# A fused retention and feed-forward kernel: another buffer and another queue for three blocks of output sums

## The chip, the cores and the metric

The kernel runs on one core of a Trainium2 chip. The metric is device time in microseconds (us) of one execution; smaller is better. The kernel before takes 835.1 us, the median of three runs (834.79 to 836.32).

## The reference

Two layers follow each other, all in float32. The first is a retention layer: for 8 batches, 8 heads, 576 positions and head size 64, the scores `q k^T / 8` are multiplied with a lower triangular matrix of powers of a decay that depends on the head, and with `v`. The second takes its output as `x`, 4608 tokens by 512:

```
a = x @ w1                     # 512 -> 1024
b = x @ w2                     # 512 -> 1024
out = ((a * b) @ w3) @ w_out   # 1024 -> 1024 -> 512
```

## The kernel before

**What is computed in which form.** The product `w3 @ w_out` (a tile called `w3o`, 1024 by 512) is made once, early. After that a block of tokens needs two large products: an "up" (`x` with `w1` and `w2`, then the elementwise product into a tile `ab`) and a "down" (`ab` with `w3o`). Both are done by a seven-product scheme (Strassen's form), so each needs sums of its operands, made by VectorE (DVE), beside the matmuls of TensorE (PE).

**Tokens.** The 4608 tokens are 12 blocks of 384, numbered m from 0. A block is cut into three pieces t of 128 tokens. One call `down(x, y)` works on two pieces, for instance x = (2, 2) and y = (3, 2): piece 2 of block 2 and piece 2 of block 3.

**What `down` does.** It makes seven products (L645) in the order 1, 7, 2, 6, 5, 4, 3, each of four matmuls, in PSUM. Product 1 is copied out by ScalarE (ACT, L679), product 2 continues in the bank of product 1, and ACT copies that too (L696). The others are added by DVE (L695, then `plus`, L649) into a tile `ot` of 128 partitions by 1024 elements. There is one buffer of `ot`. Product 3 continues in the bank of product 5, and so waits for the addition of product 5. After the additions `put` notes which rows of `ot` are whole and `store` (L723) sends them to the output. `store` takes ACT's queue unless it is told another. So the next `down` may write into `ot` only where its stores have landed, and everything that ACT has to do after a store stands behind that store's wait.

**Who fills the gaps.** `plus` also takes work out of lists that other parts filled: `spread` (sums on the weights and their sending, below), `pieces` (sums of tokens for the next stage, L966), and `aside` (among others the three sums that the next `down` needs: S3, S2, S1, lines 614, 618 and 620). One call of `plus` takes one entry of `spread` or else of `pieces`, and one of `aside`.

**The change of stage.** The first four blocks use weights that lie in SBUF (`wA`, `wS`). The later eight use a two-level form whose weight forms lie in HBM (`kept`) and come through a ring of three slots (`ra`, 896 KB each, L954). Between them, `weight_forms` makes the last sums on `wA` and `wS` (L885) and sends all forms to `kept` (L895, L898, L901), half by GpSimd (POOL), half by SyncE's queue (SP). Slots two and three of the ring lie in the space of a weight tile that has been sent, so their first loads wait for these sends to land. The first load is issued by SP (`open_first`), the second by SP (`open_second`), the third by ACT (`next_forms(nc.scalar)` near the end of the listing), and all later ones by POOL. The stage's matmuls are L1053: one `up2` for each slot.

**Order of the work around the change.** Three calls of `down` stand there, one after another in time, from about 319 to 363 us: first (1, 0) with (1, 1); second (2, 2) with (3, 2); third (3, 0) with (3, 1). After the first comes the last part of a retention chunk (`pv`, copies L306 on ACT), loads for the next chunks, and the scaling of `v` of the next chunk by its decays on ACT (L202, eight instructions). After the third come `front` (transposes L218, copies L221), `state` (L255, L259) and `score` (L233), and then the first `up2`. The order on every engine is the order in which the program is written down; the compiler adds waits on semaphores. Each DMA of SP or ACT is given one of eight semaphores in turn, each DMA of POOL one of eight others, and a DMA waits for the landing of the one that had its semaphore before.

Of the kernel before, what the change touches and what calls it, by code (L numbers as in the profile page):

```python
# [8 lines left out]
F32 = mybir.dt.float32  # L9
# [10 lines left out]
def kernel(  # L20
# [13 lines left out]
    nc = tc.nc  # L34
    moe_w1, moe_w2, moe_w3, moe_w_out = (
        w.bitcast(I32).rearrange("r (c t) -> r c t", t=2) for w in (moe_w1, moe_w2, moe_w3, moe_w_out))
    B, H, S, D = q.shape
    DM = H * D
    DF = moe_w3.shape[0]
    CV = 512  # L40
    P = 128
# [12 lines left out]
    TB = S // NB  # L54
    NT = 2 * TB // P
    KD = DM // P
    KF = DF // P
# [6 lines left out]
    ffn = ctx.enter_context(tc.tile_pool(name="ffn", bufs=2))  # L64
# [6 lines left out]
    pools = {}  # L71
# [123 lines left out]
    def scale(g, nm, scalar=False, engine=nc.gpsimd):  # L195
        c = g % NC
        sz = sizes[c]
        t, gam = live[nm, g], {"q": gq, "v": gk}[nm]
        t = t[:sz].rearrange("p (b h) d -> p b h d", b=2)
        if scalar:  # L200
            for h in range(H) if scalar is True else scalar:
                nc.scalar.mul(t[:, :, h, :], t[:, :, h, :], gam[:sz, c, h:h + 1])  # L202
            return
        engine.tensor_tensor(
            out=t, in0=t, in1=gam[:sz, c].unsqueeze(1).unsqueeze(3).to_broadcast([sz, 2, H, D]), op=ALU.mult)
# [366 lines left out]
    aside, owed, spread, beside, loads = [], [], [], [], []  # L572
    g = 0
# [31 lines left out]
    def pair_of(x, y):  # L605

        if (x, y) not in pairs:
            X, Y = tokens(*x), tokens(*y)
            a = {"A11": X[:, :NP], "A12": X[:, NP:], "A21": Y[:, :NP], "A22": Y[:, NP:],
                 "S3": Y[:, :NP], "S4": X[:, NP:]}  # L610

            def sums(nm):
                if nm == "S3":
                    nc.vector.tensor_tensor(out=a["S3"], in0=a["A11"], in1=a["A21"], op=ALU.subtract)
                elif nm == "S2":
                    forms = pools["forms"].tile([P, 2, NP, P], F32, tag="forms", name="forms")
                    a["S1"], a["S2"] = forms[:, 0], forms[:, 1]
                    nc.vector.tensor_tensor(out=a["S2"], in0=a["A22"], in1=a["S3"], op=ALU.subtract)
                else:
                    nc.vector.tensor_tensor(out=a["S1"], in0=a["S2"], in1=a["A11"], op=ALU.add)  # L620
                done.append(nm)

            done = []
            pairs[x, y] = a, done, [lambda nm=nm: sums(nm) for nm in ("S3", "S2", "S1")]
        return pairs[x, y]

    def ahead(x, y, n=3):
        todo_sums = pair_of(x, y)[2]
        for _ in range(min(n, len(todo_sums))):
            aside.append(todo_sums.pop(0))  # L630

    def down(x, y, then=None, last=False):
        a, done, left = pair_of(x, y)
        second = "first" in live
        early = second or last or g >= 2 * NC - 1
        ahead(x, y)
        while len(done) < (1 if second else 3):
            aside.pop(0)()
        ps = {}
        ot = pools["ot"].tile([P, 2, 2, DM // 2], F32, tag="ot", name="ot")  # L640

        def product(nm, A, B, on=None):
            ps[nm] = ps[on] if on else acc.tile([P, DM // 2], F32, tag="acc", name="po")
            for f in range(NP):
                nc.tensor.matmul(ps[nm], a[A][:, f, :], live["W"][B][:, f, :], start=(f == 0 and not on),  # L645
                                 stop=(f == NP - 1), skip_group_check=True)

        def plus(nm, to, sb):
            nc.vector.tensor_add(ot[:, to[0], to[1]], ps[nm], ot[:, sb[0], sb[1]])  # L649
            if spread:  # L650
                spread.pop(0)()
            elif pieces:
                pieces.pop(0)()
            if early and aside and nm != 3:
                aside.pop(0)()

        def put(m, t, row, half=slice(0, 2)):

            i, n = every[m]
            r0 = t * P  # L660
            while r0 < (t + 1) * P:
                b = r0 // TB
                e = min((b + 1) * TB, (t + 1) * P)
                r = (2 * i + b) * S + n * TB + r0 - b * TB
                stores.append((out[r:r + e - r0, half.start * DM // 2:half.stop * DM // 2],
                               ot[r0 - t * P:e - t * P, row, half].rearrange("p h d -> p (h d)")))
                r0 = e
            if not keep_stores and not second:
                store()

        C11, C12, C21, C22 = (0, 0), (0, 1), (1, 0), (1, 1)
        product(1, "A11", "B11")
        first = ot[:, 0, 0]
        if second and not steps[0]:
            first = live["spare"]
        elif second:
            first = live["first"].pop(0)
            live["first"].append(first)
        nc.scalar.copy(first, ps[1])  # L679
        if second:  # L680
            store()
            finish()
            if steps[0] and sent[0] < steps[0] + 3:
                next_forms()
        product(7, "S3", "T3")
        if second:
            multiply()
        while len(done) < 3:
            aside.pop(0)()
        if then:  # L690
            ahead(*then)
        product(2, "A12", "B21", on=1)
        nc.vector.tensor_tensor(out=a["S4"], in0=a["A12"], in1=a["S2"], op=ALU.subtract)
        product(6, "S2", "T2")
        nc.vector.tensor_add(ot[:, 0, 1], ps[6], first)  # L695
        nc.scalar.copy(ot[:, 0, 0], ps[2])  # L696
        if early:
            put(*x, 0, slice(0, 1))
            store()
        plus(7, C21, C12)  # L700
        product(5, "S1", "T1")
        plus(5, C22, C21)
        product(4, "A22", "-T4")
        plus(4, C21, C21)
        put(*y, 1)
        if second:
            store()
        product(3, "S4", "B22", on=5)
        while aside and not early:
            aside.pop(0)()  # L710
        plus(3, C12, C12)
        put(*x, 0, slice(1 if early else 0, 2))
        if last:
            store()
        while aside:
            aside.pop(0)()
# [3 lines left out]
    def store(engine=nc.scalar):  # L720
        while stores:

            engine.dma_start(*stores.pop(0))  # L723
# [125 lines left out]
    ahead((2, 0), (2, 1), 1)  # L849
    up(0, 2, NQ - 1)  # L850
    down((2, 0), (2, 1), ((0, 0), (0, 1)))
    carry(2, 2)
    weights_part.close()
# [6 lines left out]
    keep_stores.clear()  # L860
    store()
    todo = [(down, (0, 0), (0, 1)), (down, (0, 2), (1, 2))]


# [50 lines left out]
    ring, sent, steps, free = [], [0], [0], []  # L915
# [34 lines left out]
    def next_forms(engine=nc.gpsimd):  # L950
        n = sent[0]
        if n < 14 * len(groups):
            nm = NAMES.index(OPERANDS[order[n % 7]][0])
            engine.dma_start(ring[n % 3], kept[n % 14 // 7][nm])  # L954
            sent[0] += 1
# [57 lines left out]
    def finish():  # L1013
        while behind:
            behind.pop(0)()

    def multiply(most=2 * len(order)):
        while results and most:
            gr, h, f, b, z, s = results.pop(0)
            m = groups[gr][s]  # L1020
            if ("ab", *every[m]) not in live:
                live["ab", *every[m]] = ffn.tile([P, 2 * KF, TB], F32, tag="ab", name="ab")
            ab = live["ab", *every[m]].rearrange("p (q i) t -> p q i t", i=4)[:, 2 * h:2 * h + 2, 2 * f + b, :]
            v = z.rearrange("p (m s) w t -> p m s w t", s=2)[:, :, s]
            nc.vector.tensor_mul(ab, v[:, :, 0, :], v[:, :, 1, :])  # L1025
            if s == 0:
                free.append(z)
            most -= 1
# [99 lines left out]
    def work(n):  # L1128
        while n > 0 and todo:
            fn, *args = todo.pop(0)  # L1130

            nxt = next((x for x in todo if x[0] in real), None)
            if nxt and nxt[0] is down:
                if fn is down:
                    args.append(nxt[1:])
                else:
                    ahead(*nxt[1:], 1 if fn is up2 else 3)
            if g == G and not todo:
                fn(*args, last=True)
            else:  # L1140
                fn(*args)
            n -= 1
            while todo and todo[0][0] not in real:
                todo.pop(0)[0]()

    g = NC
# [49 lines left out]
    g = 2 * NC - 1  # L1196
# [3 lines left out]
    pv(g)()  # L1200
    load(g + 2, "v", nc.scalar)
    load(g + 2, "k")
    scale(g + 1, "v", True)
    open_first()
    token_forms(0)

    g = 2 * NC
    work(1)
    aside.append(lambda: scale(g, "q", True))
    work(1)  # L1210
# [55 lines left out]
    g = G  # L1266
# [44 lines left out]
```

## Time and profile before

| what | value |
|---|---|
| median of three runs | 835.1 us (834.79 to 836.32) |
| the profiled execution | 834.5 us |
| its span, from the first to the last instruction | 832.8 us |
| granted TensorE clock, mean | 1.0 |
| PE busy | 814.8 us, 98% of the span |
| DVE / ACT / POOL busy | 546.3 / 291.6 / 216.3 us |
| stores by ACT's queue, by POOL's queue | 59, 4 in all |
| a store's time from issue to landing, median | 2.3 us |

A view of the timeline has one row for instructions of one kind that follow each other: start in us from the span's start, length in us, engine, line, operation, tiles (out<-in), shape, count; in brackets, how long the engine was idle before and what ended that. ACTq and SPq are the sequencers of these engines, on which DMAs are issued. A line "DMA ... us to landing" counts from issue to landing. Since the issue is on an engine's own queue, a row of several issues includes the waits between them. PE's records overlap a little: a product starts before the modelled end of the one ahead.

### The profile page before, as it was taken

How to read it: one execution, taken by the hardware profiler on the slowest of the kernel's cores; microseconds unless marked ns; L12 is line 12 of the kernel's file. 1: busy time of each engine (PE TensorE's matmuls, PEld its weight loads, DVE VectorE, ACT ScalarE, POOL GpSimd, SP SyncE). 2: the span in 40 equal slices, each digit the busy share in tenths (PEclk: the TensorE clock that was granted, in tenths of full speed). 3: DMA queues.
4: the chain of work that ended last, by engine and by line, in shares of the span. 5: the costliest groups of instructions: out<-in, count | busy, mean ns of one | idle time of the engine just before them, and what ended most of it. 6: DMA issues, size and time to landing. Idle time of an engine off the chain costs nothing.

```text
span 832.8 us, 15818 instructions
## 1 busy us (share of the span) xinstructions
PE 814.8 (98%) x6117; PEld 733.5 (88%) x6117; DVE 546.3 (66%) x962; ACT 291.6 (35%) x609; POOL 216.3 (26%) x247
## 2 busy tenths in 40 slices
PE   7999999999999999999999999999999999999998
PEld 7888999644888998789999889998889998899987
DVE  4899999992554558754657755677745667646653
ACT  4787566581111010245443024341034331033300
POOL 1000000001103262005556005565006460045600
PEclk9999999999999999999999999999999999999999
DMA  9995464436045568998886447978245453145311
GB/s 195 228 215 138 78 153 127 123 105 112 3 80 130 86 175 276 286 282 209 202 227 184 100 85 205 232 232 222 56 92 180 162 191 114 37 150 215 138 30 46
DMA packets 197485, 126.96 MB, mean 152 GB/s; under 512 B 157849, under 2 KB 179097, under 8 KB 197409
## 3 DMA queue, kind: packets, MB, share of 16 engines
q1 hardware_dynamic: 168560, 50.40, 29.4%
q0 software_dynamic: 11824, 63.31, 23.4%
q10 hardware_dynamic: 17024, 12.23, 5.3%
q8 instruction: 48, 0.79, 0.4%
q14 instruction: 29, 0.23, 0.1%
HBM read 103.62 MB, written 22.28 MB: 151 GB/s over the span
## 4 chain that ended last, share of the span: by engine, by line
PE 81%; DVE 7%; DMA 5%; SPq 3%; issue 2%; ACT 2%; POOL 0%; ACTq 0%; DVEq 0%
PE po L645 21%; PE up L1053 17%; PE up L528 14%; PE seed L1053 13%; PE ps L477 7%; PE xps L299 3%; PE sc L233 3%; PE xps L274 1%; DMA out_dram<-ot 1%; PE st L255 1%; SPq L171 1%; DMA bl_k<-in_k_dram 1%; DVE ab L1025 1%; PE tp L218 1%; DMA kept<-wA 1%
## 5 line engine op out<-in xcount | busy, mean ns | idle before, releaser
L645 PE MATMUL po<-w3o,ab 128*128 128x256 f32 x552 | 125.4, 381 | 3.3 <-DVE ot L649 2.4
L645 PEld LDWEIGHTS po<-w3o,ab 128*128 128x128 f32 x552 | 103.6, 190 | 20.4 <-DVE ot L649 4.8
L1058 POOL TENSOR_TENSOR cc<-cc 128x384 f32<-128x384 f32 x112 | 109.3, 1002 | 3.8 <-ACT cc L1076 2.4
L1065 DVE TENSOR_TENSOR cc<-seed,cc 128x384 f32<-128x384 f32 x88 | 48.7, 553 | 69.1 <-PE seed L1053 60.1
L1053 PE MATMUL up<-xT,ra 128*128 128x192 f32 x384 | 73.6, 328 | 0.4 <-DMA ra<-kept 0.4
L181 POOL TENSOR_TENSOR bl_q<-bl_q,gqs 128x512 f32<-128x512 f32 (+1 forms) x26 | 26.0, 1020 | 184.1 <-DMA bl_q<-in_q_dram 180.5
L528 PE MATMUL up<-xT,wA 128*128 128x192 f32 x384 | 70.8, 328 | 0.3 <-ACT xT L306 0.3
L533 DVE TENSOR_TENSOR c<-up,c 128x384 f32<-128x384 f32 x80 | 44.0, 551 | 38.9 <-PE up L528 38.6
L1065 DVE TENSOR_TENSOR cc<-up,cc 128x384 f32<-128x384 f32 x88 | 48.5, 551 | 29.8 <-PE up L1053 21.8
L236 DVE TENSOR_TENSOR pm<-sc,mask 128x512 f32<-128x512 f32 (+1 forms) x80 | 45.3, 628 | 33.4 <-PE sc L233 33.3
L1053 PEld LDWEIGHTS up<-xT,ra 128*128 128x128 f32 x384 | 63.7, 190 | 1.7 <-DMA ra<-kept 0.7
L645 PE MATMUL po<-wB,forms 128*128 128x256 f32 x288 | 65.1, 379 | 0.0
L528 PEld LDWEIGHTS up<-xT,wA 128*128 128x128 f32 x384 | 63.3, 190 | 1.8 <-issue 0.7
L645 PEld LDWEIGHTS po<-wB,forms 128*128 128x128 f32 x288 | 54.7, 190 | 7.4
L1072 ACT COPY seed<-up 128x384 f32<-128x384 f32 x56 | 25.9, 463 | 100.1 <-PE up L1053 59.2
L954 POOL DMA_DIRECT2D ra<-kept x53 | 29.9, 565 | 117.7 <-PE seed L1053 88.5
L477 PE MATMUL ps<-wo,w3T 128*128 128x512 f32 x128 | 55.1, 592 | 0.0
L1053 PE MATMUL up<-ra 128*128 128x192 f32 x288 | 54.8, 326 | 0.0
L1053 PE MATMUL seed<-e,ra 128*128 128x192 f32 x256 | 50.9, 329 | 0.0
L477 PEld LDWEIGHTS ps<-wo,w3T 128*128 128x128 f32 x128 | 24.3, 190 | 30.1 <-issue 29.7
L1053 PEld LDWEIGHTS up<-ra 128*128 128x128 f32 x288 | 48.1, 190 | 0.1
L528 PE MATMUL up<-T,wS 128*128 128x192 f32 x256 | 46.7, 326 | 1.3 <-ACT e L395 1.3
(129 smaller groups left out, 1463.8 us busy)
## 6 DMA issues: line engine op xcount, KB each, us to landing
ra<-kept POOLq DMA_DIRECT2D x53, 896.0 KB, 5.1
raw<-in_moe_w_dram SPq DMA_DIRECT2D x72, 128.0 KB, 3.0
out_dram<-ot ACTq DMA_DIRECT2D x50, 128.0 KB, 2.3
bl_q<-in_q_dram SPq DMA_DIRECT2D x192, 32.0 KB, 3.3
bl_k<-in_k_dram SPq DMA_DIRECT2D x136, 32.0 KB, 3.2
raw<-in_moe_w_dram SPq DMA_DIRECT2D x16, 256.0 KB, 6.1
ld_k<-in_k_dram SPq DMA_DIRECT2D x8, 512.0 KB, 6.3
raw<-in_moe_w_out_dram SPq DMA_DIRECT2D x32, 128.0 KB, 2.7
```

What stands on the lines that cost most here:

```text
L181: nc.gpsimd.tensor_tensor(out=part, in0=part, in1=gqs[:, :, n0:n0 + n].unsqueeze(3).to_broadcast([P, NP, n, BL]), op=ALU.mult)
L233: nc.tensor.matmul(sc[j][:sz, p, :sz], kT[hs, b, p, :sz], qT[hs, b, p, :sz], start=True, stop=True)
L236: nc.vector.tensor_mul(pm[:sz, b, j, :, :sz], sc[j][:sz, :, :sz], mask[:sz, :sz].unsqueeze(1).to_broadcast([sz, NP, sz]))
L477: nc.tensor.matmul(ps, live["w3T", ft][:, g, :], live["wo"][:, g, :], start=(g == 0), stop=(g == KF - 1))
L528: nc.tensor.matmul(ps[:, w, :], a[:, w, r, :], b[:, r, :], start=(new and w == r == 0), stop=(w == r == 1), skip_group_check=True)
L533: nc.vector.tensor_add(c[:, to], ps, c[:, sb])
L645: nc.tensor.matmul(ps[nm], a[A][:, f, :], live["W"][B][:, f, :], start=(f == 0 and not on), stop=(f == NP - 1), skip_group_check=True)
L954: engine.dma_start(ring[n % 3], kept[n % 14 // 7][nm])
L1053: nc.tensor.matmul(ps[:, w, :], weight_of(slot, a, w), B[b], start=(new and w == 0), stop=True, skip_group_check=True)
L1058: nc.gpsimd.tensor_tensor(out=o, in0=o, in1=i, op=ALU.add)
L1065: nc.vector.tensor_add(c[:, j], ps, with_add[:, j])
L1072: nc.scalar.copy(p6, p1)
```

## The change

Three things are done.

- A flag `sender` is set for a call of `down` that is early enough in its stores (`early`) and comes before the first `up2` (`not steps[0]`). These are the three calls named above. Their stores inside `down` go through POOL's queue in place of ACT's.
- The call with x = (2, 2) takes its sums not into `ot`, but into a buffer of the tag `ab` in the pool `ffn`, which has two buffers of that tag; the one whose turn it is held block 1, whose tokens are through.
- The scaling of `v` for chunk 2·NC moves: it is no longer issued on ACT before the second `down`, but put into `aside` in two halves, at the head of that list, ahead of the three sums S3, S2, S1 of the third `down`.

```
+        sender = nc.gpsimd if early and not steps[0] else nc.scalar
 ...
-        ot = pools["ot"].tile([P, 2, 2, DM // 2], F32, tag="ot", name="ot")
+        if x == (2, 2):
+            ot = ffn.tile([P, 2 * KF, TB], F32, tag="ab", name="spare").rearrange("p f t -> p (f t)")
+            ot = ot[:, :2 * DM].rearrange("p (r c d) -> p r c d", r=2, c=2)
+        else:
+            ot = pools["ot"].tile([P, 2, 2, DM // 2], F32, tag="ot", name="ot")
 ...
-                store()              # in put, and at three more places in down
+                store(sender)
 ...
-    scale(g + 1, "v", True)
     open_first()
     token_forms(0)
     g = 2 * NC
+    aside.extend(lambda j=j: scale(g, "v", range(j, j + H // 2)) for j in (0, H // 2))
     work(1)
```

What this makes of the order, engine by engine: PE's and SP's instructions are the same and in the same order. ACT loses ten stores, and its eight scalings of `v` come after the second `down`'s two copies in place of before them. POOL gains these ten stores, ahead of its first ring load. On DVE, in the second `down`, the sum S3 of the third comes after the three token sums on `xT` in place of before them, and S2 and S1 come after the two sums on `e` in place of before them. On DMA semaphores: the ten stores no longer take one of the eight that SP and ACT share.

More of the change, by code (lines that the diff above doesn't have):

```diff
@@ L680, in down @@
         if second:
-            store()
+            store(sender)
             finish()
@@ L698, in down @@
             put(*x, 0, slice(0, 1))
-            store()
+            store(sender)
         plus(7, C21, C12)
@@ L706, in down @@
         if second:
-            store()
+            store(sender)
         product(3, "S4", "B22", on=5)
```

## The prediction

> **What bounds the kernel now.** I read the page first: PE is busy 98% of the span, so a change that leaves PE's work alone can only win PE's idle time, 18 us in all. The slices of the page show ACT, DVE and the DMAs crowded between 320 and 370 us. So I read PE's timeline there for its idle times, then ACT's for what held it, then the issues that follow.
>
> ```profile
> PE 814.8 (98%) x6117; PEld 733.5 (88%) x6117; DVE 546.3 (66%) x962; ACT 291.6 (35%) x609; POOL 216.3 (26%) x247
> ```
> ```profile
> 338.97 1.99 PE L645 MATMUL po<-w3o,carry 128*128 128x256 f32 x8 [1.40 <-ACT ot L679]
> ...
> 346.66 1.99 PE L645 MATMUL po<-w3o,carry 128*128 128x256 f32 x8 [0.52 <-DVE ot L649]
> ...
> 360.67 1.99 PE L645 MATMUL po<-w3o,ab 128*128 128x256 f32 x8 [1.31 <-DVE ot L649]
> ...
> 367.46 0.81 PE L1053 MATMUL up<-xT,ra 128*128 128x192 f32 x4
> ...
> 371.53 0.81 PE L1053 MATMUL up<-xT,ra 128*128 128x192 f32 x4
> ```
>
> Three stalls of PE lie in the second and third `down`, 3.23 us together. The last two lines are the starts of the first and second `up2`.
>
> ```profile
> 325.98 9.23 ACTq L723 DMA_DIRECT2D out_dram<-ot  x4
> 335.25 0.59 ACT L306 COPY xT<-xps 128x512 f32<-128x512 f32 x1 [9.30 <-DMA out_dram<-ot]
> ...
> 336.21 2.45 ACT L202 ACTIVATE ld_v<-ld_v,gk 64x128 f32<-64x128 f32 x8
> 338.56 0.36 ACT L679 COPY ot<-po 128x256 f32<-128x256 f32 x1
> ...
> 344.44 6.34 ACTq L723 DMA_DIRECT2D out_dram<-ot  x3
> 351.02 0.37 ACT L679 COPY cc<-po 128x256 f32<-128x256 f32 x1 [7.41 <-DMA out_dram<-ot]
> 357.52 0.37 ACT L696 COPY ot<-po 128x256 f32<-128x256 f32 x1 [6.13 <-DMA out_dram<-ot]
> ...
> 364.99 0.35 ACTq L954 DMA_DIRECT2D ra<-kept  x1
> ```
>
> ACT stands behind its own stores twice, and at 357.52 waits until the second block's stores have left `ot`. These cause the first and third stall. But the second `up2` needs the ring's second slot:
>
> ```profile
> 364.51 0.34 SPq L954 DMA_DIRECT2D ra<-kept  x1
> ```
> ```profile
> ra<-kept SPq DMA_DIRECT2D x1, 896.0 KB, 5.1
> ra<-kept ACTq DMA_DIRECT2D x1, 896.0 KB, 8.5
> ```
>
> It lands at 364.51 + 5.1 = 369.6, and is used at 371.53: **1.9 us of slack**. The third slot lands at 364.99 + 8.5 = 373.5, for about 376. Both loads wait for the weight sends, which fill the DMA engines (share 1.13 from 347 to 364 us).
>
> **What the change removes.** A product follows the one ahead every 1.73 us (340.80 to 344.25 holds two); after a stall the step is 1.83.
>
> - First stall. Without the four stores ACT copies `xT` from 333.9 and is free at 335.1; without the scalings ahead, product 1 is copied at about 336.0. Product 2 starts at 335.68 + 1.73 = 337.4, not 338.97: **1.56 won**.
> - Second stall. It waits for the addition of product 5. Everything is 1.56 earlier, and S3 (0.60 net of overlap) is no longer ahead of that addition. DVE: addition 6 at 341.23, 7 at 341.68, the weight sums (1.22, 0.95) to 344.03, addition 5 to 344.45. Product 3 starts at 344.5, not 346.66: 2.16 won so far; 0.2 of the stall is left.
> - Third stall. `ot` was last read by stores issued before 335 us. Even at the 7.6 us of POOL's one store here they have landed by 343, nine before they are needed. Additions follow their products; the stall of 1.31, its overlap 0.16 and a short wait of 0.1 go: **3.7 us** at the first `up2`, which would start at 363.7.
>
> **What it adds, and what hides it.** Ten stores on POOL, 0.58 each by its row (5.8 us), lie in an idle time of 42.69 that ended with its store at 364.97; its next work is a ring load at 373.95. Each waits there for its sums, and only later stores are behind it. The eight scalings (2.45) fall between 342.1 and 344.6, where ACT idles until product 1 of the third block ends near 348.2; their reader is at 363.73. S3 ends at 344.9 + 2.0 (`xT`) + 0.6 = 347.5 and is needed at 348.05; without that 0.5 margin each 0.1 costs 0.1. S2 and S1 end at 350.9, needed from 351.5. The `ab` buffer was last read at 331 and is next written after 370. Each is put at nothing.
>
> **What takes back.** By the compiled order's waits, ACT's third-slot load and SP's second-slot load both end up waiting for the same landing, the last of four 128 KB sends (issued 359.69, 4.5 later landed: 364.2). In the kernel before ACT got there late enough to stand little. Now it arrives at 361.4 and stands to about 364.6. Then come its issue 0.35, the state copy 0.58, and only then the copy of the first `up2`'s first product, at 365.5 against 364.55: 0.9 lost. The first `up2` ends at 367.46 + 4.07 − 3.7 + 0.9 = 368.7. The second slot still lands at 364.5 + 5.1 = 369.6, so the second `up2` starts at 369.7: another 1.0 lost. What is left is 371.53 − 369.7 = **1.8 us**. Later starts have slack (the third slot 1.0 to 2.6) and the listed PE waits after this are few, so I carry it to the end.
>
> The price not shown is when that send lands now. From above: SP lost 0.7 waiting on a semaphore at 352.6, and stores ahead of the sends move earlier; up to 1.0 earlier. From below: two stores of 128 KB now go ahead of it; at 309 GB/s, the rate of the same 347 to 364 us, 256 KB take 0.8: up to that much later. I take no shift, since the same bytes pass engines that are full. The gain lies between 1.0 and 2.8.
>
> Sum: 834.5 − 1.8 = 832.7 for the profiled execution. The median of runs is 0.6 above it: **833.3**.
>
> [...] Two loads of 896 KB, issued 0.48 us apart, landed 5.1 and 8.5 us after issue, that is 3.9 apart: one after the other, not shared. [...]
>
> **The rivals.**
>
> 1. *The two loads mix.* SP has two semaphore checks after the common landing, ACT three; that gives SP a lead of about 0.1 us, where the row shows order at 0.48. Against it: a 512 KB load of ACT issued 0.17 after a 256 KB send at 335.19 landed well after it. For it: a store issued at 344.44, 0.13 after a 512 KB load, landed before that load. If they share, the second slot lands between 370.8 and 372.4, the second `up2` starts 0.6 earlier to 0.9 later than before: 834.5 to 836.0.
> 2. *ACT's load goes first, and the kernel is slower.* Place: the second slot. It decides as soon as ACT's issue is ahead of SP's. The second slot then lands 8.5 after 364.6 to 365, at 373.1 to 373.5, and `up2` starts 1.7 to 2.0 later than before: 836.8 to 837.1. For it: ACT now waits there in advance; against it: one check more.
> 3. *The sends land earlier.* SP's sends are freed of waits on stores and on the 512 KB load before them. If they land 1.0 to 1.5 earlier, ACT's stand shrinks as well, and 2.6 to 3.2 are won: 832.2. Against: a DMA share over 1 leaves no room.
> 4. *The change does not do what it says.* The compiled order shows the stores on POOL and PE's order unchanged, so only its cover can fail; no chance of its own.
>
> **How the numbers follow.** My forecast has 57%, spread from 832.5 to 834.1; rival 1 has 20%, rival 2 9%, rival 3 14%. 0.2%, about what a measurement can tell from no change, is 1.7 us: faster is below 833.4. The forecast straddles it: 30 of its 57 points are below. Faster: 30 + 14 = 44%. Same: 27 + 20 = 47%. Slower: 9%. The range reaches over the forecast, rival 1 and most of rival 3: 832.2 to 836.0.
>
> **What would show it.** Right: no ACT idle behind `out_dram`; the stalls of 1.40 and 1.31 gone; first `up2` near 363.7; a new idle time of ACT ending at the issue of its ring load; a PE wait "DMA ra<-kept" at the second `up2` near 369.7. Wrong: that wait ending at 371 or later (rivals 1 and 2), or absent with the start before 369 (rival 3); a PE stall on DVE in the third `down`; a POOL store that landed so late that `ot` is waited for.

## The result, and the profile after

**838.75 us** (median of 22 runs, 835.27 to 842.13) against 835.3 us for the kernel before (median of 22, 834.34 to 838.88): a ratio of 1.0039, 95% interval 1.0029 to 1.0050. The change makes the kernel 0.4% slower; it had been forecast 1.8 us faster, at 833.3. The profiled execution took 838.66 us, its span is 837.0 us (832.8 before).

PE's timeline of the kernel after, in the stretch that the prediction spoke of (start, length, line, tiles, shape; in brackets the idle time before and what ended it):

```profile
329.32 1.99 PE L651 MATMUL po<-w3o,ab 128*128 128x256 f32 x8 [0.53 <-DVE ot L655]
...
337.73 1.89 PE L651 MATMUL po<-w3o,carry 128*128 128x256 f32 x8
...
344.73 1.99 PE L651 MATMUL po<-w3o,carry 128*128 128x256 f32 x8
...
356.92 1.89 PE L651 MATMUL po<-w3o,ab 128*128 128x256 f32 x8
...
363.28 0.81 PE L1059 MATMUL up<-xT,ra 128*128 128x192 f32 x4
363.93 0.81 PE L1059 MATMUL up<-e,ra 128*128 128x192 f32 x4
369.43 1.65 PE L1059 MATMUL seed<-e,ra 128*128 128x192 f32 x4 [4.69 <-ACT seed L1078]
...
374.71 1.13 PE L1059 MATMUL up<-xT,ra 128*128 128x192 f32 x4
```

All three stalls of the second and third `down` are gone (in this execution PE came to the first `down` 0.32 us later: 329.32 against 329.00), and the first `up2` starts at 363.28 in place of 367.46. But inside it PE stands for 4.69 us, and the second `up2` starts at 374.71, 3.2 later than before. The chain of waits says what held it:

```profile
361.54 6.16 DMA kept<-wA
...
368.02 0.35 ACTq L960
...
368.89 0.49 ACT seed L1078
...
369.43 1.65 PE seed L1059 x4
```

The last 128 KB send of weight forms was issued at 361.54 and landed 6.16 later, at 367.69 (before: issued at 359.69, landed at 364.25). ACT stood at its ring load until then, with the first `up2`'s product uncopied. A table of stretches, from 366 to 376 us, has the granted clock third from the right (PEclk), then the DMA share and GB/s:

```profile
366.00:368.00 2.00, 0.00 (x0) 0.00 (x0) 0.00 (x0) 0.00 (x0) 0.00 (x0) 1.00 0.38 109
368.00:370.00 2.00, 0.57 (x2) 0.58 (x3) 0.00 (x0) 1.37 (x3) 0.00 (x0) 0.63 0.51 151
370.00:372.00 2.00, 2.00 (x8) 2.00 (x7) 0.00 (x0) 0.83 (x3) 0.00 (x0) 0.50 1.01 394
372.00:374.00 2.00, 2.00 (x8) 2.00 (x7) 0.00 (x0) 1.18 (x4) 0.00 (x0) 0.50 0.99 377
374.00:376.00 2.00, 2.00 (x10) 2.00 (x10) 0.99 (x2) 0.13 (x1) 0.00 (x0) 0.67 0.75 97
```

PE's clock fell to half. In stretches of 0.25 us it is 0.50 from 368.51 to 375.34: from 3.8 us after PE had stopped until 5.9 us after it went on. That is why the same `up2` shows products of 1.65 and 1.13 us where others take 0.81. And the ring's two loads, by the list of DMA issues (KB each, us from issue to landing):

```profile
ra<-kept SPq DMA_DIRECT2D x1, 896.0 KB, 5.9
ra<-kept ACTq DMA_DIRECT2D x1, 896.0 KB, 7.1
```

Issued 0.13 us apart, they landed 1.3 apart (3.8 before, when they were issued 0.48 apart).

**The account** at the transposes that end this part of the stage (380.63 before, 384.12 after, +3.49): the first `up2` starts 4.18 earlier; PE stands 4.69; the rest of that `up2` takes 5.28 at half clock in place of 2.77, another 2.51; from 374.71 to 375.34 half clock costs 0.3; some 0.15 is left over. These terms say where PE lost the time, not what each would save if it were gone (e10 below). The span is 4.2 longer; the last 0.7 comes in small pieces later and was not followed.

### The profile page after: what moved, and what is told of

It is laid out like the page before. It is cut to its first block, busy times and chain, and to the rows that moved or that the text cites. A ratio compares the mean times of both kernels' runs of the same rounds, so it can differ in the third digit from the quotient of the medians.

```text
span 837.0 us, 15823 instructions
## 1 busy us (share of the span) xinstructions
PE 817.4 (98%) x6117; PEld 737.1 (88%) x6117; DVE 546.1 (65%) x962; ACT 291.4 (35%) x609; POOL 222.1 (27%) x257
## 4 chain that ended last, share of the span: by engine, by line
PE 85%; DVE 4%; DMA 4%; issue 3%; POOL 1%; ACT 1%; SPq 1%; ACTq 0%; DVEq 0%; POOLq 0%
PE po L651 24%; PE up L1059 16%; PE up L528 16%; PE seed L1059 12%; PE ps L477 7%; PE xps L299 3%; PE sc L233 3%; PE xps L274 2%; PE st L255 1%; DVE ab L1031 1%; DMA ld_q<-in_q_dram 1%; PE tp L218 1%; POOL cc L1064 1%; DMA raw<-in_moe_w_dram 1%; DMA kept<-wA 1%
## 5 line engine op out<-in xcount | busy, mean ns | idle before, releaser
L1059 PEld LDWEIGHTS up<-xT,ra 128*128 128x128 f32 x384 | 65.5, 194 | 1.1
L1078 ACT COPY seed<-up 128x384 f32<-128x384 f32 x56 | 25.9, 463 | 99.9 <-PE up L1059 56.4
L1059 PEld LDWEIGHTS seed<-e,ra 128*128 128x128 f32 x256 | 43.1, 192 | 6.2 <-ACT seed L1078 5.6
```

Of the source, the lines that this page charges most:

```text
L1059: nc.tensor.matmul(ps[:, w, :], weight_of(slot, a, w), B[b], start=(new and w == 0), stop=True, skip_group_check=True)
L1078: nc.scalar.copy(p6, p1)
```

## The experiments

Three explanations of the late send were to be told apart. **A, bytes ahead**: PE and the sums are earlier, so more stores are issued in front of the last send, on whichever queue. **B, the queue**: transfers of POOL's queue slow the others more than ACT's do. It was also to be found out whether the clock (**C**) and ACT's stand, its wait at the ring load, are causes of their own.

For the DMA side one measure serves in all: the time from the issue of the first block's first store to the landing of the last 128 KB send, one profile each, with the time (median) beside it. The experiments ran on three chips, on which the kernel before had medians of 835.8 to 836.0 us; the ratios below are to these.

| kernel | stores ahead of the last send | send landed after (us) | time (us) |
|---|---|---|---|
| before | second block, 1 of 4 of the third | 38.27, 37.95 | 835.3 |
| after (and two with its DMA order) | second block, 4 of 4 of the third | 41.12, 39.55 (39.97, 38.38) | 838.75 (837.94, 839.35) |
| e1, all on ACT's queue | second block, 1 of 4 of the third | 37.52 | 836.56 |
| e2, POOL's queue alone | second block | 37.70 | 840.1 |
| e5, third late | second block | 37.43 | 837.28 |
| e11, third late, slot 3 by SP | second block | 38.33 | 836.61 |
| e12, the same, second by ACT | second block | 39.87 | 836.24 |
| e6, e7, both late | none | 36.63, 36.60 | 836.32, 833.73 |

Sorted by the bytes of these stores: none, 36.6; 512 KB, 37.4 to 39.9; 640 KB, 37.5 to 38.3; 1024 KB, 38.4 to 41.1. The ends are apart, as A wants; in the middle single profiles scatter by more than 512 KB are worth.

**e1: stores back on ACT's queue**

```
-        sender = nc.gpsimd if early and not steps[0] else nc.scalar
+        sender = nc.scalar
```

> The changed kernel with the ten stores back on ACT's queue; the `spare` buffer and the moved scalings of v stay. Theory A (bytes ahead): in the changed kernel the last send of weight forms landed at 367.69 us in place of 364.25 because three stores of 128 KB of the third block are now issued ahead of it, whichever queue they are on; ACT stood at its ring load to 368.02, PE stood 4.69 us, and its granted clock was 0.50 from 368.5 to 375.4. The stalls of the second and third `down` stay away here as well, the stores are as early, so the send lands at 367 to 368 and the time is 837.5 to 839.5. Theory B (the queue): transfers of POOL's queue are what slows the others; then the send lands at 364 to 366, PE stands under 3 us with the clock at 1.00, and the time is 833 to 836.

Measured: 836.56 us (835.27 to 838.47); against before 1.0006 [0.9994, 1.0018]. The send landed at 363.81, as B says, yet the run does not show B: PE stood elsewhere, and the stores were not as early.

```profile
364.15 1.78 PE L233 MATMUL sc<-qT,kT 64*64 64x64 f32 x32 [3.14 <-ACT qT L221]
```
```profile
360.43 2.71 ACTq L729 DMA_DIRECT2D out_dram<-ot  x2
363.18 0.65 ACT L221 COPY kT<-tp 128x256 f32<-128x256 f32 x2 [7.93 <-DMA out_dram<-ot]
```

ACT's copies of kT and qT stand behind its own stores. The first of the two waits for a sum that ends at 360.80, the last, by the trace's semaphore events, until 362.64 for the landing of a weight send; it goes out at 362.66. Both are issued behind the last send (359.94), so only one store of the third block is ahead of it, as in the kernel before. So the buffer and the moved scalings alone win nothing that could be measured: without POOL's queue the wait moves to `score`.

**e2: the queue alone** (`ot` for all three blocks, scalings where they were)

```
-        if x == (2, 2):
+        if False:
...
+    scale(g + 1, "v", True)
     open_first()
...
-    aside.extend(lambda j=j: scale(g, "v", range(j, j + H // 2)) for j in (0, H // 2))
```

> The kernel before with only the queue of the ten stores changed: all three blocks use `ot`, the scalings of v are where they were. The last store of the first block landed 6.4 us after its issue on POOL's queue (2.9 on ACT's before), so the second `down` must wait for `ot` until about 341.8 and not 338.1. Theory A (bytes ahead): PE loses some 3 us there, the third block's stores are then as late against the sends as before, the send lands at 364 to 366, no long stand of PE at the first `up2`: 835 to 838. Theory B (the queue slows the other transfers): the send lands at 366 to 368 in spite of the later stores, and stalls add up: 838 to 842.

Measured: 840.1 us (839.31 to 841.17), 1.0049 [1.0034, 1.0064]. The wait for `ot` was as expected, but longer:

```profile
343.47 3.78 PE L651 MATMUL po<-w3o,carry 128*128 128x256 f32 x8 [4.22 <-ACT ot L685]
```

A store of POOL's queue issued at 336.79 landed 6.2 us later (the one in its place in the kernel before took 3.3, not the 2.9 of the expectation); with one buffer PE pays that. A row of x8 that takes 1.99 elsewhere took 3.78: the clock was 0.50 here too, from 341.86 to 348.69. The send came 37.70 us after the first store, not later than before, although POOL's queue carried the second block's stores. By its time alone the run fits B; by the landing, of one profile, it speaks against B.

**e5 and e6: the stores of the third block, or of the second and third, held back** and issued by SP behind its load of the second slot

```
+        sender = nc.scalar if not early or steps[0] else None if x in [(2, 2), (3, 0)] else nc.gpsimd   # e5: only (3, 0)
...
-        while stores:
+        while engine and stores:
...
     next_forms(nc.scalar)
+    store(nc.sync)
```

> The changed kernel, but the third block's stores (512 KB) are held back and issued by SP after its load of the ring's second slot, behind the sends. Theory A (bytes ahead): 384 KB less ahead of the last send at 280 to 300 GB/s is 1.3 us; it lands at 366 to 366.4, PE stands about 3.3 us in place of 4.69, and as the clock fell 3.7 us after PE had stopped, it mostly stays at 1.00, which saves another 3.0: 833.5 to 835.5. Theory B (POOL's queue slows the other transfers): the two earlier blocks' stores are still on it, the gain is at most those of the third: 836 to 838.

> As the one before, but the stores of the second block (512 KB, from the `spare` buffer, next written at 385 us) are held back too: seven stores by SP after its load of the second slot. Theory A (bytes ahead): 896 KB less ahead of the last send is 3.0 us: it lands at 364 to 365, ACT is let go at about 364.7, PE stands about 1 us at the first `up2`, the second slot lands near 370 and the second `up2` starts there, 1.5 before the kernel before: 833 to 834.5, provided that the stores behind the ring load delay nothing. Theory B (POOL's queue): only the first block's three stores are on it; about the same time, so this run only tells whether either holds. Against both: if the sends are paced by something else than bytes (their own issue, the loads of 256-byte packets), the send still lands after 366.5 and the time is above 836.

Measured: e5 837.28 us, 1.0017 [1.0005, 1.0029]; e6 836.32 us, 1.0006 [0.9996, 1.0016]. The sends came as much earlier as A wants: 36.63 in e6, 3.1 less than the mean of the four profiles with the changed kernel's order (39.75), for 1024 KB held back, of which 896 had been counted (3.0 expected). In e6 PE stands only 0.19 us behind ACT. But both were slower than expected, for the place of the stand moved to the ring's second slot:

```profile
372.23 0.99 PE L1059 MATMUL up<-xT,ra 128*128 128x192 f32 x4 [2.93 <-DMA ra<-kept]
```
```profile
ra<-kept SPq DMA_DIRECT2D x1, 896.0 KB, 7.2
ra<-kept ACTq DMA_DIRECT2D x1, 896.0 KB, 8.7
```

Freed by the same landing, ACT issues its load 0.13 after SP's, and the second slot takes 7.2 us in place of 5.1. This is the prediction's first rival, but perhaps not all of it: with ACT's load as close, and no held-back stores directly behind on SP's queue, the slot took 5.9 to 6.0 us in three profiles (after, e10, e13); with four such stores it took 6.9 (e5), with seven 7.2 (e6).

**e7: as e6, and the third slot's load by SP too**

```
-    next_forms(nc.scalar)
+    next_forms(nc.sync)
```

> The changed kernel with the stores of the second and third block issued by SP behind its ring loads, and the third slot's load issued by SP behind the second's. With ACT issuing it 0.13 us after SP's, the second slot took 7.2 us to land (372.09), in the kernel before, 0.48 apart, 5.1. Theory G (the two loads share the DMA engines when they are issued together): here the second slot lands 5.1 to 5.5 us after its issue, at 370 to 370.5 by the clock of that run, PE stands under 1.5 us there, its clock stays at 1.00, and the time is 832.5 to 834, the lowest of all. Rival (the ring load is slow for another reason, the stores of SP behind it for instance): it lands after 371.5 as before, and the time is 835.5 to 837.

Measured: **833.73 us** (832.08 to 838.8) against 835.89 of the kernel before on the same chip: 0.9980 [0.9964, 0.9995]. It is the only version here that is faster than both. In the profiled execution, one of its fastest (832.25), the second slot's load landed in 4.7 us with nothing of ACT beside it, and PE stands 0.58:

```profile
ra<-kept SPq DMA_DIRECT2D x1, 896.0 KB, 4.7
```
```profile
363.01 0.81 PE L1059 MATMUL up<-xT,ra 128*128 128x192 f32 x4
...
367.88 0.89 PE L1059 MATMUL up<-xT,ra 128*128 128x192 f32 x4 [0.58 <-DMA ra<-kept]
```

The clock is 1.00 throughout. So G holds, and e6 against e7 is worth 2.6 us. The one word between them moves two things: ACT's load no longer goes beside the second slot's, and SP's stores come behind the third slot's load and no longer directly behind the second's. The first alone, without held-back stores, is 5.9 to 6.0 us for the slot (after, e10, e13) against 4.7 (e3, below). Whether the stores make the rest, up to 7.2, was not tried apart.

**e3: the changed kernel with only that word changed**

> The changed kernel with the load of the ring's third slot issued by SP, after that of the second, in place of ACT. ACT no longer stands at it. Theory E (the late sends decide, and ACT's stand only shows it at another place): the sends land as late, so the second slot lands 5.1 us after about 367.9, at 373.0; the first `up2` runs through from 363.3 to 367.4, PE then stands 5.6 us at the second `up2`, the clock is 0.50 for some 6 us after, and the time is 838.5 to 840. Theory F (ACT's stand is the cause): 834 to 836. Also: with the two loads in one queue, the second slot lands within 5.5 us of its issue in place of 5.9 to 7.2.

Measured: 839.35 us (835.78 to 841.24), 1.0036 [1.0020, 1.0051], no better than the changed kernel: E. ACT's stand is not a cause of its own; with the sends late, PE waits for the slot instead. Its profiled execution is its fastest (835.78, PE stood 2.41 us there), so it shows the place and not the median.

**e10: PE kept busy in the stand**

```
         product(p5, "S1", "T1", True)
+        if steps[0] == 1:
+            t = acc.tile([P, P], F32, tag="acc", name="idle")
+            for _ in range(16):
+                nc.tensor.matmul(t, ident, ident, start=True, stop=True)
```

> The changed kernel with 16 needless products of `ident` on PE in front of the first product that stands at the first `up2` (they add work whose result nobody reads). They fill some 3.5 of its 4.69 us with matmuls, and all later work starts when it did. Theory C (the clock is a part of its own): the clock fell to 0.50 since PE had stood for 3.7 us, and stayed there until 375.4; with PE busy it stays at 1.00, the transposes after the stage's first part start 3.0 earlier (381.1 and not 384.1), and the time is 835.2 to 836.5 against 838.75. Theory D (the loss is the late send and the stand alone, and the clock costs nothing that is not hidden): within 1 us of the changed kernel.

Measured: 837.94 us (835.93 to 839.77), 1.0024 [1.0012, 1.0036]. That is 0.8 below the changed kernel, or 1.4 if each is taken against the kernel before beside it; not the 3.0 of C. The clock did stay at 1.00 in the profile, and PE shows where the rest went:

```profile
364.64 3.73 PE L1085 MATMUL idle<-ident 128*128 128x128 f32 x32
368.33 0.92 PE L1059 MATMUL seed<-e,ra 128*128 128x192 f32 x4
...
372.88 0.89 PE L1059 MATMUL up<-xT,ra 128*128 128x192 f32 x4 [1.68 <-DMA ra<-kept]
```

(The x32 are records of 16 products.) At full clock the first `up2` is through sooner, and then waits for the second slot. Of the 2.8 us that half clock takes in the changed kernel (2.51 + 0.3 in the account), only what reaches past that slot's landing (373.83, plus 0.14 as here) counts: 374.71 − 373.97 + 0.3 = 1.0. **The second slot bounds, as the prediction had it; the clock adds about 1.**

**e11 and e12: only the third block late, slot 3 by SP; then the second block's stores on ACT's queue in place of POOL's**

```
-        sender = nc.gpsimd if early and not steps[0] else nc.scalar
+        sender = nc.scalar if not early or steps[0] else None if x == (3, 0) else nc.gpsimd       # e11
+        sender = nc.scalar if not early or steps[0] or x == (2, 2) else None if x == (3, 0) else nc.gpsimd   # e12
```

> The changed kernel with the third slot's load by SP behind the second's, and only the third block's stores behind them on SP; the second block's 512 KB leave by POOL's queue at once, as in the changed kernel. From the first store of the first block to the landing of the last 128 KB send it took 36.6 us with both blocks late, 37.4 with the third late, 38.4 to 41.1 with neither (one profile each, three for the last). Theory A (bytes ahead): 512 KB more ahead of the sends than with both late, at 280 to 300 GB/s up to 1.8 us: this stretch is 37.4 to 38.4, and the time 0.5 to 1.8 above the 833.7 of both late: 834.2 to 835.5. Rival: the second block's stores are long through, their bytes cost nothing, 833.2 to 834.2.

> As the one before, with the three stores of the second block on ACT's queue in place of POOL's: ready at the same times, the same bytes, only the queue differs. Theory A (bytes ahead, whichever queue): within 0.7 us of the one before in time, and its last send lands within 1 us of it. Theory B (POOL's queue slows the other transfers more than ACT's does): the last send lands 1 to 2 us earlier and the time is 1 to 2 lower. A wait of ACT behind these stores could cost up to 1 us of PE's time in the second `down`; it would show as a stall of PE there.

Measured: e11 836.61 us (832.11 to 837.84), 1.0006 [0.9994, 1.0019]; e12 836.24 us (832.82 to 838.4), 1.0000 [0.9984, 1.0017]. In e11 the send is 1.7 later than in e7, for 512 KB more ahead of it (up to 1.8 expected), and the time 2.9 more: more than expected, since PE stood 2.29 us at the second `up2` and the clock fell again. With the third slot's load on SP throughout, the medians follow what is held back: 839.35 us (e3, nothing), 836.61 (e11, 512 KB), 833.73 (e7, 1024 KB). **That is the firmest sign that the stores ahead of the sends cost the time**, for it rests on 11 or 12 runs each and not on single profiles.

Whether the queue matters too is told by e11 and e12, between which only the queue of the second block differs: they are 0.4 us apart in time, and the send is later with ACT (39.87 against 38.33), not earlier, though e12's profile is of one of its slowest executions (838.03). **B finds no support**: no run shows a gain by leaving POOL's queue. But the runs of each of the two spread over more than 5 us, so a small effect of the queue is not excluded. No stall of PE in the second `down` came of ACT's wait.

**e13 and e14: both kernels once more, for a second profile**

> The changed kernel unaltered, for a second profile of it. Theory A and the clock: last send of 128 KB 38.4 to 41.1 us after the first block's first store; PE stands at the first `up2` for some 2.5 to 4.7 us; where it stands under about 3.5 the clock stays at 1.00 and the time is under 837.5, else it is 838 to 840.

> The kernel before unaltered, for a second profile. In its first profile the last send landed 38.3 us after the first block's first store, and the second slot 1.9 us ahead of its use. Theory A: 37.5 to 39.3 here, the second `up2` late by under 1 us or not at all, 834.5 to 836.5. If the landing varies by 2 us or more in this kernel too, the difference between the two kernels' profiles is in part a matter of the execution.

Measured: e13 839.52 us, send after 39.55 us; PE stood 3.11 us, the clock was 0.50 from 371.06 to 374.47. So the expectation on the clock (1.00 under 3.5 us, an estimate from the 3.7 us after which it fell in the changed kernel) is wrong. e14 836.96 us, send after 37.95; and the clock fell in the kernel before as well, after stands of only 0.31 and 0.66 us:

```profile
362.00:364.00 2.00, 1.69 (x19) 1.22 (x18) 1.97 (x6) 1.49 (x6) 0.00 (x0) 1.00 1.12 356
364.00:366.00 2.00, 1.34 (x40) 1.21 (x40) 1.12 (x4) 1.18 (x4) 0.58 (x1) 1.00 1.09 310
366.00:368.00 2.00, 2.00 (x33) 1.70 (x30) 1.33 (x4) 0.61 (x2) 0.00 (x0) 0.57 1.10 324
368.00:370.00 2.00, 2.00 (x5) 1.13 (x4) 0.16 (x1) 0.00 (x0) 0.00 (x0) 0.57 0.92 337
```

Before the drop, PE was busy 1.69 and 1.34 of 2 us, with small products (transposes, `state`, `score`).

## Why the prediction was wrong

- **What is removed: right.** Product 2 was won 1.56 us and is (338.97 − 337.73 + 0.32 for the start of this execution). Product 3: 2.16 predicted, 2.25 measured. First `up2`: 3.7 predicted, 4.18 + 0.32 = 4.50 measured; 0.3 of the difference lies in transposes, `state` and `score` (4.54 us from the transposes to `up2`, 4.87 before) where ACT's copies no longer stand behind stores.
- **What hides the additions: right in that nothing of POOL, DVE or the scalings stalls PE.** The ten stores on POOL were each issued as their sums were ready.
- **The step that failed: "I take no shift" for the landing of the last send**, with bounds of 1.0 earlier and 0.8 later. It came 3.4 later in the profile (2.9 counted from the first block's first store). So ACT, which was to be let go at 364.6, stood until 368.02, and PE, for which 0.9 had been put down, stood 4.69. The list of issues between 352 us and the last sends, before and after, shows the miscount:

```profile
kept<-wA SPq DMA_DIRECT2D x4, 128.0 KB, 4.6
out_dram<-ot ACTq DMA_DIRECT2D x1, 128.0 KB, 4.1
```
```profile
out_dram<-ot POOLq DMA_DIRECT2D x4, 128.0 KB, 5.8
kept<-wA SPq DMA_DIRECT2D x4, 128.0 KB, 5.8
```

  Three more stores of 128 KB are ahead and not two: 384 KB, 1.3 us at 280 to 300 GB/s (the mean from 333 us to the landing of the last send: 280 after, 298 before). (The one of before was issued 0.08 us behind the last send and landed 0.4 ahead of it.) The four profiles with this DMA order average 39.75 us to the landing, the two of before 38.1: 1.65 in the mean, about what the bytes ask, and the profile on record lies another 1.4 above. The prediction argued that "the same bytes pass engines that are full". That is true of the total and wrong of the order: earlier stores move in front of what PE waits for.

  But these three stores are not the whole delay. SP was already late at the first of its last eight sends, when only one store of the third block had been issued, at 352.61 (before, then after):

```profile
350.93 3.60 SPq L895 DMA_DIRECT2D kept<-wA  x4
```
```profile
352.80 3.49 SPq L901 DMA_DIRECT2D kept<-wA  x4
```

  Counted from the first store that is 25.0 us (25.2 in e14) against 26.2 (25.8, 25.9 and 25.1 in e13, e10 and e3): 0.7 of the 1.65 in the mean. Nor did the engines move the same bytes per us: from 24 to 33 us after the first store it was 261 GB/s in the profile on record, 284, 276 and 335 in e13, e10 and e3, and 305 and 302 in the kernel before; of the four with one order, the higher the rate, the earlier the send. What sets this rate, and whether the second block's stores, some 2.4 us earlier than before, hold SP up, stays open.
- **"The second slot still lands 5.1 after its issue": wrong.** It took 5.9. The prediction's first rival named the mixing of the two loads, with a lead of SP of about 0.1 us (0.13 measured), and priced it at up to 0.9 slower, on the old landing of the send. Added to a late send it goes past the range: 367.89 + 5.9 = 373.8 for the slot, 2.3 after the old start of the second `up2`.
- **What no step had: the clock.** About 1 us by e10. The prediction's range ended at 836.0, since each rival was priced with the others' causes at zero; late send (1.65 in the mean, 2.9 in the profile), mixing (0.8 on the slot) and clock (1) came together here, at one late landing for which SP, ACT and PE all stood waiting. The rival with which the slower side was argued (ACT's load first) didn't happen in the changed kernel: SP's was first.

That the two loads land one after the other was read from one row, with a lead of 0.48 us. It held at leads of 0.48 and 0.50 (before, e14): 5.1 and 5.3 us for the first. It did not hold at smaller ones: issued 0.13 us apart the loads landed 1.1 to 1.7 apart (after, e5, e6), and in e1, issued 0.03 apart (ACT's first), 0.2 apart, 8.2 and 8.3 us after issue. Why so little lead decides was not tried.

## What to carry to other kernels

Where DMA engines are full (share 1.03 to 1.17 from 345 to 362 us here, before and after), a store that is freed earlier can be a transfer moved ahead of the one that somebody waits for: list what is issued in front of the awaited transfer, before and after, and count the bytes. Here the time that PE had gained counted only when results that nobody waits for were held behind the loads of the next stage, and the two large loads, of which one is needed first, were on one queue (e7); either alone did not do it (e6, e3). And price a stand of PE with the half clock that may come with it (in nine of 13 profiles here; about 1 us of the changed kernel's time), and rivals together where one event brings them all.

## What the runs showed of the hardware

- **Half clock came in two lengths.** Read in stretches of 0.25 us around the change of stage (20 to 30 us of each profile), 0.50 lasted 3.41 us in each of six profiles (e1, e5, e6, e11, e13, e14) and 6.83, twice that, in three (after, e2, e12). The long one came with stands of 4.04, 4.22 and 4.69 us (e12, e2, after), five of the short ones with stands of 2.29 to 3.14; stands of 0.58, 1.68 and 2.41 (e7, e10, e3) brought none there. (The mean clock of the span, 0.990 in e13 and 0.996 in e3, is lower than these stretches give, so these two had more half clock elsewhere.) In the three long ones PE still stood 0.92 to 1.61 us after the drop, in the six short ones 0.25 at most. The single stand doesn't decide: 2.29 us brought a drop in e11 and 2.41 none in e3; in the 3.41 us ahead of the drop PE had stood 2.03 us in e11, and in e14 only 0.97, the rest being small products. In e11 the drop came at 372.58, when PE had been at work again since 371.20. What sets the two lengths, and what brings the drop, was not shown.
- Of 81 executions of the kernel before beside the experiments, 53 had a mean clock of 0.999 or more (median 835.6 us) and 28 less (836.8); of the 22 of the kernel after none reached 0.999, of e7 eight of twelve.
- The landing of one and the same send varied by 2.7 us between executions with the same DMA order (38.38 to 41.12). One profile of such a stretch is not enough to price it.
